# Routing of three batches in a fused attention and mixture-of-experts kernel: element-by-element operations moved from VectorE to GpSimd

## The chip, the cores and the metric

The kernel runs on one core of one Trainium2 chip. The metric is device microseconds (us) for one execution of the whole program. The engines are named as in the profile: PE (TensorE matmul), PEld (its weight loads), DVE (VectorE), ACT (ScalarE), POOL (GpSimd) and SP (SyncE, which only issues DMAs here).

## The reference

Attention with rotary embedding over 4 batches, 8 heads, 576 positions, head size 64; its output, laid out as rows of 512, goes through a router and eight experts. Each token uses one expert, weighted by its probability.

```python
x = attn_out.transpose(0, 2, 1, 3).reshape(B, S, H * D)
logits = np.einsum('bsd,de->bse', x, w_gate)
local_gate = sigmoid(np.einsum('bsd,de->bse', x, w_local))
for b in range(B):
    prev_e = -1
    for s in range(S):
        fresh_e = argmax(logits[b, s])
        e = fresh_e if s == 0 or local_gate[b, s] < 0.5 else prev_e
        prev_e = e
        p = softmax(logits[b, s])
        out[b, s] = p[e] * (relu(x[b, s] @ w1[e]) @ w2[e])
```

## The kernel before

**Attention.** Sixteen pairs of heads are walked in 144 softmax steps, nine to a pair. In a step DVE takes the row minimum `mn` of the scores (L272), PE writes the scores `s` of the next step (L267, two buffers), ACT takes the exponential `e` (L289), PE transposes an earlier `e` (`tm`, L325), ACT copies the transposed tile to its high half `pth` (L303), DVE subtracts it to get the low half `ptl` (L307), and PE multiplies both by the values (`pv`, L361), which ACT and DVE take out to `xt` (L371, L372). Five of the transposed tiles are split by POOL instead (`ON_POOL`, L298 to L300). POOL also does the rotary products (L196, L197) and the splits of queries, keys and values (L206 to L213).

**Routing.** The rows of logits of the first three batches are done together (`route(0, B - 1)`, 15 blocks of 128 tokens), while the last pairs of heads are still in attention; the fourth batch is routed later, under the experts. The parts of the routing are generators; the string `ORDER` gives each a softmax step: `f` finds the expert of each token from the logits (`mx`, `d`, `ex`, `c8`, `f`) and whether it starts anew (`rs`), `r` and `R` carry the last choice forward along the sequence (a transpose `row` and a scan), `e` brings the experts back (`ec`, `e`) and counts them (`cnt`, `oha`, `cox`), `k` ranks each token within its expert (`rk`, `lb`, `lc`, and the one-hot rows `ohr` on POOL), `s` and `p` make the probability, `l`, `x`, `c` plan the first six tiles of 128 tokens, `t` marks which token stands in which slot (`c`, `ex`), `g` gathers their numbers with fifteen matmuls (`idx`, then `ihi`, `gidx`, `ipad`, `sidx` on DVE), `G` issues indirect DMAs that gather the rows of the first four tiles (`x`, L915, on POOL's queue), and `0` and `1` split the first expert weights on POOL (`w_m`, `w_q`, L854 and L855).

**Hand-over.** When attention is done, PE transposes the first gathered tile (`tx`, L926) and starts the products of the experts. From there to the end it is PE that sets the time: `h` (L940) and `o` (L983) follow each other without a gap that matters until the last scatter.

**What sets the order.** PE's order is the order of the code. On DVE, ACT and POOL a scheduler places the instructions at build time; each engine then works through its own list in order, so an instruction that waits holds up all that stand behind it on its engine.

Of the kernel before, what the change touches and what calls it, by code (L numbers as in the profile page):

```python
# [17 lines left out]
ALU = mybir.AluOpType  # L18
# [35 lines left out]

ORDER = ".....fs.rRe.klx.c0pt...wg.1.G"
BIG = 4096.0
# [10 lines left out]
for _n, _w in (  # L67
    ("iota128", 128), ("code8", 8), ("p1", 1),
    ("keys", NBLK * NE), ("s0", NBLK), ("pad", NBLK), ("tok64", NBLK),
    ("scan0", 8 * NG + 8), ("tile128", 25),  # L70
):
    _COLS[_n] = (_off, _off + _w)
    _off += _w
# [3 lines left out]
def _constants():  # L77
# [14 lines left out]
    tok64 = np.zeros((P, NBLK))  # L92
    s0 = np.zeros((P, NBLK))
    pad = np.zeros((P, NBLK))
    s0[0, ::NB] = 1
    pad[:64, 4::NB] = 64
# [5 lines left out]
    put("keys", (TWO23 + 8 * tok[:, :, None] + 7 - np.arange(8)).reshape(P, -1))  # L102
    put("s0", s0)
    put("pad", pad.astype(np.int32))
# [33 lines left out]
def tile_attention_moe(ctx, tc, qk, v, tabs, turn, consts, tri, wg, wts, out):  # L138
# [333 lines left out]
    def route(b0, nb):  # L472

        n = nb * NB
        cs = slice(b0 * NB, b0 * NB + n)
        final = b0 + nb == B
        st = {}

# [3 lines left out]
        def fresh():  # L482
            if final:
                scores(b0)
                yield
            lg = lg_all[:, 0:n]
            mx = blk("mx")
            dve.tensor_reduce(mx, lg[:, :, 0:8], axis=AX.X, op=ALU.max)
            yield
            d = blk("d", 8)  # L490
            dve.tensor_tensor(d, lg[:, :, 0:8], bc(mx, 2, 8), op=ALU.subtract)
            yield
            ex = blk("ex", 8)
# [12 lines left out]
            key = blk("key")  # L506
            dve.tensor_tensor(key, rs, f, op=ALU.mult)
            yield
            st.update(ex=ex, key=key)

# [21 lines left out]
        def experts():  # L532
# [10 lines left out]
            oh = oha[:, cs]  # L543

            dve.tensor_scalar(tcode[:, cs], e, -7.0, 4096.0, op0=ALU.add, op1=ALU.mult)
            cnt = small([P, NE, NG + 1], "cnt", BF16)
            dve.tensor_tensor(cnt[:, :, 1:n + 1].rearrange("p e j -> p j e"), bc(C["code8"], 1, n), bc(e, 2, 8), op=ALU.is_equal)
            dve.tensor_tensor(oh, bc(C["code8"], 1, n), bc(e, 2, 8), op=ALU.is_equal)

            if b0 == 0:  # L550
                dve.memset(cnt[:, :, 0], 0.0)
            else:
                dve.tensor_copy(cnt[:, :, 0], cox_t[0][:, :, NG])
                if n < NG:
# [19 lines left out]

        def probs():
# [15 lines left out]
        def ranks():  # L591
# [45 lines left out]
    def slots(codes, nblk, first, n):  # L637

        st = {}

        def spread_tokens():
# [6 lines left out]
            rhs = rhs.rearrange("p (c j n) -> p c j n", n=n, c=2)  # L648
            dve.tensor_tensor(w, bc(codes(), 1, nblk), bc(tcode[:, 0:nblk], 2, n), op=ALU.is_equal)
# [711 lines left out]
```

## Time and profile before

| what | value |
|---|---|
| median of 3 runs | 546.08 us (544.13 to 546.13) |
| profiled execution: time | 546.83 us |
| profiled execution: span, first to last instruction | 545.1 us |
| granted TensorE clock, mean | 0.994 |
| busy share of the span: PE, DVE, ACT, POOL | 96%, 71%, 63%, 60% |
| routing of the first three batches | about 250 to 293 us |
| first transpose of the experts (`tx`) | 299.62 us |

The busy shares are means over two halves with different limits: in attention, up to about 300 us, PE and DVE are both nearly full; among the experts PE alone is. What a change to the routing does is read in the stretch from 250 to 300 us.

### The profile page before, as it was taken

The page shows a single profiled execution, that of the slowest core. Times are in us where ns is not written, and L with a number is a line of the kernel's source. Part 1 is how long each engine was busy: PE and PEld are TensorE (multiplying, and loading weights), DVE is VectorE, ACT ScalarE, POOL GpSimd, SP SyncE. Part 2 cuts the span into 40 slices and gives each one's busy share as a digit, 9 for nine tenths or more (in the row PEclk, how much of TensorE's full clock was granted, in tenths as well). Part 3 has the DMA queues.
Part 4 walks back from the last instruction along what each step waited for, and adds up shares of the span by engine and source line. Part 5 has one row for each costly group of instructions (what it writes and reads, how often), then busy time and mean ns, then how long its engine had stood idle before and what let it go on. Part 6 is the DMA issues. An engine that isn't in the chain of part 4 may idle for free. (4 is left out here: it accounts for less than half of the span.)

```text
span 545.1 us, 10718 instructions
## 1 busy us (share of the span) xinstructions
PE 521.0 (96%) x3281; PEld 460.4 (84%) x3281; DVE 388.3 (71%) x724; ACT 344.7 (63%) x766; POOL 327.9 (60%) x243
## 2 busy tenths in 40 slices
PE   7989999999999999999999999999999999999992
PEld 3788999999999999998888788887888887888881
DVE  6898999999999999999999935428422635421630
ACT  2799898888998999987676623353523443442440
POOL 2996989878787989887498401337511455411332
PEclk9999999999999999999999999999999999999997
DMA  8759588766877787895289305371647494737340
GB/s 264 284 125 239 166 241 241 152 200 196 245 179 213 204 223 185 209 252 132 57 157 272 86 21 174 115 272 45 227 102 246 123 342 102 247 99 232 87 167 25
DMA packets 63322, 97.37 MB, mean 179 GB/s; under 512 B 28113, under 2 KB 38353, under 8 KB 61458
## 3 DMA queue, kind: packets, MB, share of 16 engines
q1 hardware_dynamic: 60210, 86.84, 56.6%
q0 software_dynamic: 3040, 9.71, 5.5%
q8 instruction: 28, 0.46, 0.4%
q14 instruction: 44, 0.36, 0.2%
HBM read 76.98 MB, written 12.86 MB: 165 GB/s over the span
## 5 line engine op out<-in xcount | busy, mean ns | idle before, releaser
L983 PE MATMUL o<-w,hs 128*128 128x512 f32 x456 | 113.5, 398 | 0.2 <-ACT hs L964 0.2
L272 DVE TENSOR_REDUCE mn<-s 128x1 f32<-128x576 f32 x144 | 107.5, 747 | 3.6 <-PE s L267 2.2
L289 ACT ACTIVATE e<-s,mn 128x576 f32<-128x576 f32 x128 | 95.1, 743 | 18.9 <-DVE mn L272 15.4
L940 PE MATMUL h<-w,xs 128*128 128x512 f32 x444 | 106.2, 393 | 0.9 <-DVE xs L307 0.5
L267 PE MATMUL s<-m,qst 128*128 128x288 f32 x512 | 97.5, 311 | 5.4 <-ACT e L289 3.0
L307 DVE TENSOR_TENSOR ptl<-tm,pth 128x512 fp32r<-128x512 f32 x139 | 95.1, 685 | 6.4 <-ACT pth L303 4.0
L940 PEld LDWEIGHTS h<-w,xs 128*128 128x128 f32 x444 | 82.6, 188 | 19.1 <-DVE w L885 1.2
L983 PEld LDWEIGHTS o<-w,hs 128*128 128x128 f32 x456 | 83.0, 188 | 17.6 <-ACT hs L964 0.6
L989 POOL DMA_INDIRECT out_dram<-os,sidx x19 | 22.8, 1201 | 124.8 <-ACTq L891 71.4
L303 ACT CAST pth<-tm 128x512 fp32r<-128x512 f32 x139 | 80.8, 581 | 12.3 <-PE tm L325 11.2
L267 PEld LDWEIGHTS s<-m,qst 128*128 128x128 f32 x512 | 74.7, 189 | 12.1 <-ACT e L289 6.1
L325 PE MATMUL tm<-wid,e 128*128 128x128 f32 x512 | 77.1, 273 | 1.3 <-ACT e L289 0.5
L196 POOL TENSOR_TENSOR stage<-stage 128x1152 f32<-128x1152 f32 x26 | 68.9, 2665 | 14.0 <-DMA stage<-in_qk_dram 11.9
L361 PE MATMUL pv<-pth,v 128*128 128x288 f32 x256 | 76.4, 314 | 0.4 <-DVE ptl L307 0.2
L361 PE MATMUL pv<-ptl,v 128*128 128x288 f32 x256 | 76.6, 315 | 0.0
L325 PEld LDWEIGHTS tm<-wid,e 128*128 128x128 f32 x512 | 62.0, 140 | 2.2 <-DVE ptl L307 1.0
L885 DVE TENSOR_TENSOR w<-stage,w 128x1024 fp32r<-128x1024 f32 x37 | 50.7, 1403 | 15.7 <-SPq L1049 7.2
L361 PEld LDWEIGHTS pv<-pth,v 128*128 128x128 f32 x256 | 48.3, 189 | 2.8 <-DVE ptl L307 0.9
L361 PEld LDWEIGHTS pv<-ptl,v 128*128 128x128 f32 x256 | 48.4, 189 | 0.0
L307 DVE TENSOR_TENSOR xs<-tx,xs 128x512 fp32r<-128x512 f32 x19 | 13.1, 689 | 41.8 <-ACTq L891 32.2
L307 DVE TENSOR_TENSOR hs<-th,hs 128x512 fp32r<-128x512 f32 x26 | 17.5, 688 | 29.5 <-ACTq L891 17.8
L197 POOL TENSOR_TENSOR stage<-stage 128x576 f32<-128x576 f32 x26 | 36.9, 1432 | 0.2
(198 smaller groups left out, 817.3 us busy)
## 6 DMA issues: line engine op xcount, KB each, us to landing
stage<-in_wts_dram SPq DMA_DIRECT2D x84, 512.0 KB
stage<-in_qk_dram SPq DMA_DIRECT2D x13, 1152.0 KB
qst<-xq SPq DMA_DIRECT2D x56, 128.0 KB
stage<-in_v_dram SPq DMA_DIRECT2D x16, 320.0 KB
m<-xq SPq DMA_DIRECT2D x14, 288.0 KB
m<-xk SPq DMA_DIRECT2D x14, 288.0 KB
m<-xq SPq DMA_DIRECT2D x14, 256.0 KB
m<-xk SPq DMA_DIRECT2D x14, 256.0 KB
```

The costliest lines, as they stand in the source:

```text
L196: engine.tensor_tensor(x, x, tab[:, 2 * f:2 * f + 2], op=ALU.mult)
L197: engine.tensor_tensor(rr[:, f], x[:, 0], x[:, 1], op=ALU.add)
L267: pe.matmul(st[:, h, lo:hi], lhs, keys[:, k0:k0 + hi - lo], start=(n == 0), stop=(n == len(parts_) - 1))
L272: dve.tensor_reduce(mn, s_t[g][:, :, 0:HALF], axis=AX.XY, op=ALU.min)
L289: act.activation(dst.rearrange("p (h s) -> p h s", h=2), s_t.pop(g)[:, :, 0:HALF], AF.Exp, bias=mn, scale=-1.0, accum_out=sums[:, col:col ...
L303: act.copy(hi, src)
L307: dve.tensor_tensor(lo, src, hi.bitcast(F32), op=ALU.subtract)
L325: pe.transpose(ps[:, k], src[:, k * P:(k + 1) * P], ident)
L361: pe.matmul(pv_t[p, u], lhs.rearrange("p c d -> p (c d)"), rhs, start=(n == 0), stop=(n == 9))
L885: (pool if k in on_pool else dve).tensor_tensor(lo, src, hi.bitcast(F32), op=ALU.subtract)
L940: pe.matmul(ps[:, c], xs_t[t][:, x, k], w[y][:, c * 512:(c + 1) * 512], start=(k == 0 and n == 0), stop=(k == 3 and n == 2))
L983: pe.matmul(ps, hs_t[t][:, x, k], w[y][:, (k % 2) * 512:(k % 2 + 1) * 512], start=(k == 0 and n == 0), stop=(k == 7 and n == 2))
```

## The change

Within the routing of the first three batches, operations that go element by element and read SBUF alone are issued on POOL; the reductions, the scans, whatever reads PSUM, and the short chain that plans the tiles stay on DVE. A fused instruction becomes two on POOL (compare, then multiply). One addition goes to ACT. Two parts are cut in two, so that what uses a result of POOL stands a softmax step later: `F` (maximum and key) after `f`, and `E` (the scan of the counts) after `e`. Both take free places of `ORDER`; the other parts keep theirs. The fourth batch stays on DVE.

```diff
-ORDER = ".....fs.rRe.klx.c0pt...wg.1.G"
+ORDER = ".....fFsrReEklx.c0pt...wg.1.G"
...
+        some = dve if final else pool
...
-            dve.tensor_tensor(d, lg[:, :, 0:8], bc(mx, 2, 8), op=ALU.subtract)
+            some.tensor_tensor(d, lg[:, :, 0:8], bc(mx, 2, 8), op=ALU.subtract)
...
-            dve.scalar_tensor_tensor(c8, d, 0.0, keys, op0=ALU.is_equal, op1=ALU.mult)
-            dve.scalar_tensor_tensor(rs, lg[:, :, 8], ZTHR, C["s0"][:, cs], op0=ALU.is_lt, op1=ALU.max)
-            yield
+            if final:
...
+            else:
+                pool.tensor_scalar(c8, d, 0.0, None, op0=ALU.is_equal)
+                pool.tensor_tensor(c8, c8, keys, op=ALU.mult)
+                pool.tensor_scalar(rs, lg[:, :, 8], ZTHR, None, op0=ALU.is_ge)
+                pool.tensor_tensor(rs, rs, C["later"][:, cs], op=ALU.mult)
+            yield
+            st.update(ex=ex, c8=c8, rs=rs)
+
+        def resets():
+            c8, rs = st["c8"], st["rs"]
             f = blk("f")
             dve.tensor_reduce(f, c8, axis=AX.X, op=ALU.max)
             yield
             key = blk("key")
-            dve.tensor_tensor(key, rs, f, op=ALU.mult)
...
+                pool.tensor_tensor(rs, rs, f, op=ALU.mult)
+                pool.tensor_tensor(key, f, rs, op=ALU.subtract)
...
-            dve.tensor_scalar(tcode[:, cs], e, -7.0, 4096.0, op0=ALU.add, op1=ALU.mult)
-            dve.tensor_tensor(cnt[:, :, 1:n + 1].rearrange("p e j -> p j e"), bc(C["code8"], 1, n), bc(e, 2, 8), op=ALU.is_equal)
-            dve.tensor_tensor(oh, bc(C["code8"], 1, n), bc(e, 2, 8), op=ALU.is_equal)
+            if not final:
+                whole, e, far = e, blk("p"), blk("c8", 8)
+                pool.tensor_copy(e, whole)
+                pool.tensor_tensor(far, bc(C["code8"], 1, n), bc(e, 2, 8), op=ALU.subtract)
+            for x in (cnt[:, :, 1:n + 1].rearrange("p e j -> p j e"), oh):
+                if final:
+                    dve.tensor_tensor(x, bc(C["code8"], 1, n), bc(e, 2, 8), op=ALU.is_equal)
+                else:
+                    pool.tensor_scalar(x, far, 0.0, None, op0=ALU.is_equal)
+            some.tensor_scalar(tcode[:, cs], e, -7.0, 4096.0, op0=ALU.add, op1=ALU.mult)
...
+        def counts():
+            cnt = st["cnt"]
             cox = small([P, NE, NG + 1], "cox", BF16, bufs=2)
...
-            dve.tensor_scalar(se, se, 1e-9, None, op0=ALU.add)
+                act.add(se, se, 1e-9)
...
-            dve.tensor_tensor(p, p, st["se"], op=ALU.mult)
+            some.tensor_tensor(p, p, st["se"], op=ALU.mult)
...
-            dve.tensor_tensor(o, r, hi, op=ALU.subtract)
+            some.tensor_tensor(o, r, hi, op=ALU.subtract)
...
+                pool.tensor_scalar(hi, hi, -TWO23, None, op0=ALU.add)
+                pool.tensor_tensor(tcode[:, cs], hi, tcode[:, cs], op=ALU.add)
                 for j in range(n):
                     pool.tensor_scalar(ohr[:, b0 * NB + j], C["iota128"], o[:, j:j + 1], None, op0=ALU.is_equal)
             yield
-            dve.scalar_tensor_tensor(tcode[:, cs], hi, -TWO23, tcode[:, cs], op0=ALU.add, op1=ALU.add)
...
+            if first == 0:
+                far = small([P, nblk * n], "d").rearrange("p (j n) -> p j n", n=n)
+                pool.tensor_tensor(far, bc(codes(), 1, nblk), bc(tcode[:, 0:nblk], 2, n), op=ALU.subtract)
+                pool.tensor_scalar(w, far, 0.0, None, op0=ALU.is_equal)
...
-            dve.tensor_tensor(rhs[:, 0], w, bc(C["tok64"][:, 0:nblk], 2, n), op=ALU.mult)
-            dve.tensor_scalar(rhs[:, 1], w, C["p1"], None, op0=ALU.mult)
+            some.tensor_tensor(rhs[:, 0], w, bc(C["tok64"][:, 0:nblk], 2, n), op=ALU.mult)
+            some.tensor_scalar(rhs[:, 1], w, C["p1"], None, op0=ALU.mult)
```

DVE's list becomes 14 instructions shorter, POOL's 21 longer, ACT's one longer. Three places of the lists show how they move.

**DVE, start of the routing.** Before, from the maximum `mx` of the logits to the second softmax minimum behind it:

```order
L488 TENSOR_REDUCE mx_4214<-lg_all 128x15
L501 SCALAR_TENSOR_TENSOR rs_4222<-lg_all,cst 128x15
L430 RECIPROCAL sum_3604<-sum_3604 128x10
L491 TENSOR_TENSOR d_4216<-lg_all,mx_4214 128x120
L272 TENSOR_REDUCE mn_4231<-s_4194 128x1
L499 SCALAR_TENSOR_TENSOR c_6_4220<-d_4216,cst 128x120
L307 TENSOR_TENSOR ptl_3983<-tm_4201,pth_3982 128x4x128
L504 TENSOR_REDUCE f_4224<-c_6_4220 128x15
L567 TENSOR_REDUCE se_4273<-ex_4218 128x15
L507 TENSOR_TENSOR key_4226<-rs_4222,f_4224 128x15
L272 TENSOR_REDUCE mn_4280<-s_4233 128x1
```

Now, the same place (`c_6` is `c8`, written by POOL; `ex` is written by ACT from `d`, which POOL writes):

```order
L489 TENSOR_REDUCE mx_4214<-lg_all 128x15
L430 RECIPROCAL sum_3604<-sum_3604 128x10
L272 TENSOR_REDUCE mn_4229<-s_4194 128x1
L591 TENSOR_REDUCE se_4310<-ex_4218 128x15
L515 TENSOR_REDUCE f_4271<-c_6_4220 128x15
L307 TENSOR_TENSOR ptl_3983<-tm_4201,pth_3982 128x4x128
L272 TENSOR_REDUCE mn_4279<-s_4231 128x1
```

Four instructions have left the stretch, and `f`, which reads what POOL writes, now stands ahead of the `ptl` and the `mn`.

**DVE, the counts.** Now, from the experts `e` to the second `mn` behind them (`cnt` and `d`, the products of probabilities, come from POOL):

```order
L555 SCALAR_TENSOR_TENSOR e_4411<-ec_4405,cst 128x15
L372 TENSOR_TENSOR xt_4338<-pv_1_4369,tmp_4339 64x288
L272 TENSOR_REDUCE mn_4457<-s_4427 128x1
L583 SCALAR_TENSOR_TENSOR cox_4452<-cst,cnt_4413 128x128
L607 TENSOR_REDUCE p_4748<-d_4746 128x15
L307 TENSOR_TENSOR pkl_4290<-tk_4441,pkh_4289 128x256
L272 TENSOR_REDUCE mn_4516<-s_4459 128x1
```

Before, `tcode`, `cnt`, `oha` and `cox` stood between `xt` and the first `mn`, and `p` stood behind the second.

**POOL, towards the gathers.** Now, from the split of the last values to the gathers of the first four tiles (`w_m`, `w_q` are the first expert weights):

```order
L213 TENSOR_TENSOR v_15_4342<-stage,v_15_4342 128x10x64
L681 TENSOR_TENSOR d_4793<-code_4684,tcode 128x90
L682 TENSOR_SCALAR c_30_4791<-d_4793 128x90
L687 TENSOR_TENSOR ex_4792<-c_30_4791,cst 128x90
L688 TENSOR_SCALAR ex_4792<-c_30_4791,cst 128x90
L889 TENSOR_SCALAR w_m<-stage 128x1024
L890 TENSOR_TENSOR w_m<-stage,w_m 128x1024
L889 TENSOR_SCALAR w_q_4915<-stage 128x1024
L890 TENSOR_TENSOR w_q_4916<-stage,w_q_4915 128x1024
L950 DMA x_4926<-rows_d,gidx 128x513 x4
```

The four instructions between the values and the weights are new here; ahead of them, around the `ohr` of the ranks, stand three more new ones (`lc`, `lb`, `tcode`).

## Rows read from the trace of the kernel before

**Rows 1.** Windows: busy time of each engine (and instructions), clock, DMA share, GB/s.

```profile
250.00:261.00 11.00, 9.41 (x69) 7.99 (x66) 10.78 (x24) 7.96 (x21) 5.79 (x6) 1.00 0.59 135
261.00:272.00 11.00, 10.19 (x80) 9.46 (x80) 10.47 (x25) 7.66 (x18) 5.78 (x7) 1.00 0.16 29
272.00:290.00 18.00, 16.95 (x122) 15.20 (x122) 17.69 (x48) 12.12 (x31) 17.62 (x24) 1.00 0.83 196
```

**Rows 2.** Timeline of PE: start, duration, instruction, and the idle time before it.

```profile
253.69 0.80 PE L267 MATMUL s<-m,qst 128*128 128x288 f32 x4 [0.94 <-ACT e L289]
...
268.14 1.03 PE L267 MATMUL s<-xk,qtail 128*128 128x288 f32 x6 [0.81 <-issue]
```

**Rows 3.** Timeline of DVE, the four longest routing instructions that leave it.

```profile
250.47 1.36 DVE L501 SCALAR_TENSOR_TENSOR rs<-lg_all,cst 128x15 f32<-128x15 f32 x1
...
264.14 1.16 DVE L545 TENSOR_SCALAR tcode<-e 128x15 f32<-128x15 int32 x1
...
271.42 0.99 DVE L607 TENSOR_TENSOR lc<-rk,lb 128x15 f32<-128x15 f32 x1
...
283.25 0.99 DVE L652 TENSOR_TENSOR ex<-c,cst 128x90 bf16<-128x90 bf16 x1
```

**Rows 4.** Timeline of POOL in the same stretch.

```profile
249.38 0.27 POOL L468 TENSOR_TENSOR lg_all<-gm 128x45 f32<-128x45 f32 x1
...
249.62 0.67 POOL L206 TENSOR_SCALAR xq<-stage 128x576 fp32r<-128x576 f32 x1
250.38 1.42 POOL L207 TENSOR_TENSOR xq<-stage,xq 128x576 fp32r<-128x576 f32 x1
...
263.98 1.28 POOL L300 TENSOR_TENSOR ptl<-stage,pth 128x512 fp32r<-128x512 f32 x1
266.06 0.51 POOL L577 TENSOR_TENSOR d<-ex,oha 128x120 f32<-128x120 f32 x1 [0.79 <-DVE oha L548]
...
272.52 8.75 POOL L612 TENSOR_SCALAR ohr<-cst,lc 128x128 bf16<-128x128 f32 x15
...
282.64 0.25 POOL L728 TENSOR_SCALAR after<-take 128x8 f32<-128x8 f32 x1
```

**Rows 5.** Timeline of DVE: `f`, the scan of the counts, and the minimum behind it.

```profile
253.55 0.27 DVE L504 TENSOR_REDUCE f<-c 128x15 f32<-128x120 f32 x1
...
265.91 0.42 DVE L558 TENSOR_TENSOR_SCAN cox<-cst,cnt 128x128 bf16<-128x128 f32 x1
266.36 0.76 DVE L272 TENSOR_REDUCE mn<-s 128x1 f32<-128x576 f32 x1
```

**Rows 6.** Timeline of POOL up to the first gather.

```profile
285.73 1.05 POOL L854 TENSOR_SCALAR w_m<-stage 128x1024 fp32r<-128x1024 f32 x1
286.86 2.38 POOL L855 TENSOR_TENSOR w_m<-stage,w_m 128x1024 fp32r<-128x1024 f32 x1
...
290.34 2.36 POOL L855 TENSOR_TENSOR w_q<-stage,w_q 128x1024 fp32r<-128x1024 f32 x1
293.02 1.26 POOL L915 DMA_INDIRECT x<-rows_d,gidx  x1 [0.32 <-DVE sidx L672]
```

**Rows 7.** Timeline of DVE, the numbers that the gathers need.

```profile
292.20 0.53 DVE L668 CAST gidx<-ihi 128x6 uint32<-128x6 f32 x1
...
292.83 0.17 DVE L672 SCALAR_TENSOR_TENSOR sidx<-ipad,ihi 128x6 uint32<-128x6 f32 x1
```

**Rows 8.** Timeline of PE at the hand-over to the experts.

```profile
290.41 0.53 PE L661 MATMUL idx<-ex,ohr 128*128 128x12 bf16 x15
...
293.75 0.37 PE L361 MATMUL pv<-pth,v 128*128 128x288 f32 x1 [0.22 <-DVE ptl L307]
...
299.62 0.60 PE L926 MATMUL tx<-wid,x 128*128 128x128 f32 x4
```

**Rows 9.** Gathers `x`, issue to landing: the third, then the fifth and sixth.

```profile
DMA to landing us min/median/max: 5.5/5.5/5.5
...
DMA to landing us min/median/max: 3.7/3.7/3.7
```

More of the change, by code (lines that the diff above doesn't have):

```diff
@@ L68 @@
     ("iota128", 128), ("code8", 8), ("p1", 1),
-    ("keys", NBLK * NE), ("s0", NBLK), ("pad", NBLK), ("tok64", NBLK),
+    ("keys", NBLK * NE), ("later", NBLK), ("pad", NBLK), ("tok64", NBLK),
     ("scan0", 8 * NG + 8), ("tile128", 25),
@@ L92, in _constants @@
     tok64 = np.zeros((P, NBLK))
-    s0 = np.zeros((P, NBLK))
+    later = np.ones((P, NBLK))
     pad = np.zeros((P, NBLK))
-    s0[0, ::NB] = 1
+    later[0, ::NB] = 0
     pad[:64, 4::NB] = 64
@@ L102, in _constants @@
     put("keys", (TWO23 + 8 * tok[:, :, None] + 7 - np.arange(8)).reshape(P, -1))
-    put("s0", s0)
+    put("later", later)
     put("pad", pad.astype(np.int32))
@@ L498, in fresh @@
             keys = C["keys"].rearrange("p (j e) -> p j e", e=NE)[:, cs]
-            dve.scalar_tensor_tensor(c8, d, 0.0, keys, op0=ALU.is_equal, op1=ALU.mult)
             rs = blk("rs")
-            dve.scalar_tensor_tensor(rs, lg[:, :, 8], ZTHR, C["s0"][:, cs], op0=ALU.is_lt, op1=ALU.max)
+            if final:
+                dve.scalar_tensor_tensor(c8, d, 0.0, keys, op0=ALU.is_equal, op1=ALU.mult)
+                dve.scalar_tensor_tensor(rs, lg[:, :, 8], ZTHR, C["later"][:, cs], op0=ALU.is_ge, op1=ALU.mult)
+            else:
[3 more added lines that the diff above has]
+                pool.tensor_tensor(rs, rs, C["later"][:, cs], op=ALU.mult)
             yield
+            st.update(ex=ex, c8=c8, rs=rs)
+        def resets():
+            c8, rs = st["c8"], st["rs"]
             f = blk("f")
@@ L506, in fresh @@
             key = blk("key")
-            dve.tensor_tensor(key, rs, f, op=ALU.mult)
+            if final:
+                dve.scalar_tensor_tensor(key, rs, 0.0, f, op0=ALU.is_equal, op1=ALU.mult)
+            else:
+                pool.tensor_tensor(rs, rs, f, op=ALU.mult)
+                pool.tensor_tensor(key, f, rs, op=ALU.subtract)
             yield
-            st.update(ex=ex, key=key)
+            st["key"] = key
         def last_reset(part):
@@ L556, in experts @@
             yield
+            st["cnt"] = cnt
+        def counts():
+            cnt = st["cnt"]
             cox = small([P, NE, NG + 1], "cox", BF16, bufs=2)
@@ L562, in experts @@
             cox_t[b0] = cox
-            st["cnt"] = cnt
         def sums():
@@ L568, in sums @@
             yield
-            dve.tensor_scalar(se, se, 1e-9, None, op0=ALU.add)
+            if final:
+                dve.tensor_scalar(se, se, 1e-9, None, op0=ALU.add)
+            else:
+                act.add(se, se, 1e-9)
             yield
@@ L606, in ranks @@
             yield
-            dve.tensor_tensor(o, r, hi, op=ALU.subtract)
+            some.tensor_tensor(o, r, hi, op=ALU.subtract)
             if final:
                 dve.tensor_tensor(ohr[:, cs], bc(C["iota128"], 1, n), bc(o, 2, P), op=ALU.is_equal)
-            else:
+                yield
+                dve.scalar_tensor_tensor(tcode[:, cs], hi, -TWO23, tcode[:, cs], op0=ALU.add, op1=ALU.add)
+            else:
+                pool.tensor_scalar(hi, hi, -TWO23, None, op0=ALU.add)
+                pool.tensor_tensor(tcode[:, cs], hi, tcode[:, cs], op=ALU.add)
                 for j in range(n):
@@ L613, in ranks @@
             yield
-            dve.scalar_tensor_tensor(tcode[:, cs], hi, -TWO23, tcode[:, cs], op0=ALU.add, op1=ALU.add)
-            yield
-        parts = [fresh, lambda: last_reset(0), lambda: last_reset(1), experts, ranks]
+        first, second = (lambda: last_reset(0)), (lambda: last_reset(1))
         if final:
-            return parts[:4] + [sums, probs] + parts[4:] + later()
-        order = dict(f=fresh, r=parts[1], R=parts[2], e=experts, k=ranks, s=sums, p=probs, **early())
+            return [fresh, resets, first, second, experts, counts, sums, probs, ranks] + later()
+        order = dict(f=fresh, F=resets, r=first, R=second, e=experts, E=counts, k=ranks, s=sums, p=probs, **early())
         return [None if c == "." else order[c] for c in ORDER]
@@ L639, in slots @@
         st = {}
+        some = pool if first == 0 else dve
         def spread_tokens():
```

5 lines of the change are left out of this document (4 added, 1 removed).

## The prediction

> **What bounds the kernel now.** I read the busy table first, then the windows, then the waits, then the timelines of the engines from 250 to 300 us. Among the experts PE runs without a gap that matters, so what happens before 300 us is kept to the end unless something at the hand-over takes it back. In the routing stretch DVE is the fullest engine: 10.78 of 11.00 us, 10.47 of 11.00, 17.69 of 18.00 [rows 1]. PE there has idle time: 1.59, 0.81 and 1.05 us, together 3.45 us [rows 1]. The two longest gaps stand in front of a score product: 0.94 us, ended by an exponential `e` on ACT, which follows a late minimum on DVE, and 0.81 us [rows 2]. So the most that a faster DVE can give back before the hand-over is about 3.4 us.
>
> DVE is full partly because it waits while it is counted busy. Four instructions of 15 or 90 elements a row take 1.36, 1.16, 0.99 and 0.99 us [rows 3], where the same kind takes 0.17 us elsewhere (`sidx` [rows 7]). `rs` ends at 250.47 + 1.36 = 251.83, and POOL's L207 at 250.38 + 1.42 = 251.80; `tcode` ends at 265.30, POOL's L300 at 263.98 + 1.28 = 265.26 [rows 3, 4]. An instruction of DVE with operands in SBUF alone, issued while POOL is at a tile, ends with POOL's instruction. The ones that leave DVE are such instructions, so the change takes the right ones from it.
>
> **The change part by part.** I follow the order of time.
>
> *Fresh experts.* From DVE go `rs` (1.36 us), `d`, `c8` and `key`, in all some 1.7 us of its time. But `f` now stands in front of `ptl` and `mn` on DVE and waits for `c8` from POOL. POOL ends `lg_all` at 249.65 and then does `rs` (two instructions), L206, `d`, L207 and `c8` (two), in this order. Prices on POOL: a small single-input instruction 0.25, a small two-input one 0.27, one of 128x120 with two inputs 0.51, L206 0.67, L207 1.42 [rows 4]; the single-input one of 128x120 I put at 0.3, between 0.25 and the 0.58 of one `ohr` (8.75 / 15 [rows 4]). Sum: 0.25 + 0.27 + 0.67 + 0.51 + 1.42 + 0.3 + 0.51 = 3.9, so `c8` is there at about 253.6. Before, `f` started at 253.55 [rows 5]. DVE thus spends the 1.7 us waiting, and the `ptl` that used to stand ahead of `f` comes behind it. Gain here: 0, bounds +0.6 us of loss (one `ptl`) and 0.9 of gain (the gap at 253.69, if POOL is quicker).
>
> *Counts.* Three instructions of DVE (`tcode` alone 1.16 us) leave the place between `xt` and `mn`, so this `mn`, which started at 266.36 [rows 5], can start some 2 us earlier. Behind it `cox` waits for `cnt` from POOL. There the cast of `e` gets in just ahead of the L300 of 263.98, whose 1.28 us then pass, and then come `far` (0.51), `tcode` (0.25) and `cnt` (0.3 to 0.58): `cnt` stands at about 265.26 + 0.25 + 0.51 + 0.25 + 0.4 = 266.7, `cox` ends near 267.1 where it ended at 266.33 [rows 4, 5]. The matmuls of the ranks come 0.45 us later, but the gap of 0.81 us behind them closes, since the exponential it hung on is 2 us earlier. Then `p` waits for POOL's `d` (0.3 + 0.51 later) and holds up the next `mn` by some 0.7 us. Net on PE: 0.4 us gained, bounds -0.4 and +0.8.
>
> *Ranks to slots.* `lc` (0.99 us), and later both `ex`, leave DVE, which hereby comes about 1 us earlier through the dense stretch of the tile plans, and another 2 us near 283 to 287. PE has 1.05 us of idle time there [rows 1] and can take up most of it: 0.9 us, bounds 0.4 and 1.05. So PE reaches the matmuls of `idx`, at 290.41 before [rows 8], about 1.3 us earlier.
>
> *POOL's list.* In 272 to 290 POOL is busy for 17.62 of 18.00 us [rows 1], one instruction behind the other, and at its end stand the weights `w_m`, `w_q` and then the first gather [rows 6]. New in this list are `lc`, `lb` and `tcode` (0.27 + 0.25 + 0.27), and `far`, `c` and twice `ex` (0.4 + 0.27 + 0.4 + 0.3 to 0.58; a two-input one of 90 I put between the 0.27 for 45 elements of `lg_all` and the 0.51 for 120). Sum 2.3 us, bounds 2.0 and 2.6. Nothing covers it: the copy by ACT that the last L300 ahead of `ohr` waits for follows the same exponentials as before, so the start moves by half a microsecond at most. `w_q` ends at 290.34 + 2.36 + 2.3 = 295.0, and the first gather, which went out at 293.02, goes at about 295.3 with its old gap of 0.3 [rows 6]. This is the price of the change. `idx` itself has its `ex` at about 288, before PE wants it.
>
> *Hand-over.* `tx` waits for three things. PE's own list: 299.62 - 1.3 = 298.3. The first tile `x`: 295.3 plus 3.7 us (a gather with none ahead of it) or 5.5 us (the third in a row) [rows 9]. The first has none ahead but shares the DMA queues with loads of weights; I take 4.6, the middle, so 299.9, and with the start of the weight load about 300.1. Last, DVE: `gidx`, `ipad` and `sidx` have their operands in SBUF alone, and behind them on DVE stands the `ptl` for which the last `pv` wait [rows 7, 8]. They come at about 291 now, into the middle of POOL's weights, where before only the end of one caught `gidx` (0.53 us, until 292.73 [rows 7]). If `gidx` waits for the end of `w_m` (291.7) and `ipad` for the first half of `w_q` (292.7), `sidx` gets through at 293.0, where it was; if `sidx` is caught as well, it ends at 295.2, 2.2 us later. I take the first for the sum. The latest of the three decides: 300.1 against 299.62.
>
> **Sum.** Gain before the hand-over 0 + 0.4 + 0.9 = 1.3 us; it turns into a wait in front of `tx`, which starts 0.5 us later than before: +0.5 us. The profiled execution took 546.83 us (span 545.1), 0.75 above the median of the runs shown; against the median it gives 546.08 + 0.5 = 546.6 us.
>
> **A rule to weigh.** The rows above show DVE's small instructions ending with POOL's [rows 3, 4]. The Trainium skill, "SBUF — State Buffer", section "Who interferes with whom", says why: GpSimd and VectorE share one pair of SBUF ports, held for a whole instruction, and a VectorE instruction that copies or scales in a 2-port mode, or has two inputs in SBUF, blocks until GpSimd's is through. By that rule all three instructions of the index chain are caught, and the sum would be +2.2 us, 548.3; this is rival C.
>
> **The rivals.**
>
> *A, the forecast: gains given back at the hand-over.* From -1.3 (PE's own list decides because the gather lands early) to +1.3 us (5.5 us to landing: 300.8). Chance 0.62.
>
> *B, faster: the time of DVE comes through.* For it: DVE is the fullest engine in all three windows, and the waits on POOL's tiles fall away. Against it: DVE waits for POOL at `f`, `cox` and `p`. It decides if POOL gets `c8` out before 252.5, that is if small instructions cost half as much there, and if the list to the gather grows by less than 1 us. Then PE's 3.45 us come back, less up to 1: -3.4 to -1.5 us, 542.7 to 544.6. Chance 0.15.
>
> *C, slower: the index chain is caught behind POOL's weights.* `sidx` ends at 295.2, the `ptl` behind it 0.7 us later, and `pv`, at 293.75 before, starts at 295.9; `tx` comes 5.87 us behind it as before [rows 8], at 301.8: +2.2 us, and up to +3.3 if the new list of POOL is 1 us longer than I put it. For it: every case in rows 3. Against it: no row shows two such instructions in a row under a full POOL. It decides if `gidx` starts before the first half of `w_q` does. 548.3 to 549.4. Chance 0.23.
>
> *D, no effect.* That DVE's time is off the path is no case of its own: it ends in A, near 0.
>
> **How the numbers follow.** I put the point at A's 546.6. The range takes in the larger part of B and all but the top of C: 543.8 to 549.2. About 0.5%, 2.7 us, is what a measurement of this kernel can tell from no change. Faster by more than that: B's upper part and a little besides, 0.12; slower by more: the upper half of C and a little, 0.16; within: 0.72.
>
> **What would show it.** Right: in the profile after, `f` has idle time in front of it that POOL ends; `cox` and `p` too; the gap of PE at 253.69 stays near 1 us in some form, that at 268 shrinks; the first gather goes out 2 to 2.6 us after 293.02; PE waits in front of `tx` or in front of the last `pv`. Wrong: `f` starts before 252.7; POOL has idle time between `ohr` and the gather; or `tx` starts before 298.5.

## The result and the profile after

| what | before | after |
|---|---|---|
| median of all runs | 545.07 us (12 runs) | 548.4 us (12 runs, 547.06 to 550.49) |
| profiled execution: time, span | 546.83, 545.1 us | 548.26, 546.4 us |
| granted TensorE clock, mean | 0.994 | 0.992 |

The changed kernel takes 1.0058 times as long as the one before, 95% interval [1.0045, 1.0071]: slower by 3.3 us, where the prediction said 0.5. The time lies inside its range (543.8 to 549.2 us), but a slowdown of more than 2.7 us had only a chance of 0.16. That it lies inside is in part luck: the forecast started from 546.08 us, a median of three runs, and over twelve the kernel before takes 545.07; as a change, the range ended at +3.1 us. The slowdown is above all of rival A's range (-1.3 to +1.3 us) and at the top of rival C's (+2.2 to +3.3), though not by C's way, as the rows below show. One run of the kernel before, timed beside e9 to e11, took 732.72 us at a mean granted clock of 0.654 and is in no ratio.

The two profiles don't start the routing at the same moment: `lg_all`, its first instruction on POOL, stands at 247.96 in the trace after and at 249.38 in the one before [rows 4]. Rows below are quoted as they are; where I compare, I add these 1.42 us and say "shifted".

**The routing stretch.** Windows of the changed kernel, the columns as in [rows 1]:

```profile
250.00:261.00 11.00, 9.28 (x67) 7.80 (x66) 8.50 (x17) 8.03 (x21) 6.65 (x9) 1.00 0.63 143
261.00:272.00 11.00, 10.26 (x78) 9.31 (x77) 8.39 (x22) 7.92 (x19) 8.28 (x15) 1.00 0.17 21
272.00:290.00 18.00, 17.77 (x146) 16.29 (x145) 16.74 (x45) 14.76 (x36) 17.59 (x28) 1.00 0.85 207
...
308.00:312.00 4.00, 2.61 (x13) 1.50 (x14) 3.68 (x9) 1.69 (x4) 0.04 (x1) 1.00 0.23 69
312.00:316.00 4.00, 4.00 (x13) 2.86 (x14) 2.50 (x3) 0.00 (x0) 0.00 (x0) 0.57 0.01 2
```

DVE (third pair of numbers) is busy for 8.50, 8.39 and 16.74 us instead of 10.78, 10.47 and 17.69 [rows 1], and for 8.35, 8.39 and 16.87 us in windows moved by the 1.42 us; POOL (fifth) stays full in the third window. The two windows below the dots are spoken of further down. DVE's timeline shows where the freed time went:

```profile
252.28 0.28 DVE L515 TENSOR_REDUCE f<-c 128x15 f32<-128x120 f32 x1 [1.74 <-POOL c L506]
...
265.74 0.42 DVE L583 TENSOR_TENSOR_SCAN cox<-cst,cnt 128x128 bf16<-128x128 f32 x1 [2.10 <-POOL cnt L568]
266.42 0.28 DVE L607 TENSOR_REDUCE p<-d 128x15 f32<-128x120 f32 x1 [0.26 <-POOL d L604]
...
289.55 1.29 DVE L703 CAST gidx<-ihi 128x6 uint32<-128x6 f32 x1
290.76 0.16 DVE L705 TENSOR_SCALAR ipad<-ihi 128x6 f32<-128x6 f32 x1
290.95 0.89 DVE L707 SCALAR_TENSOR_TENSOR sidx<-ipad,ihi 128x6 uint32<-128x6 f32 x1
...
302.73 4.43 DVE L920 TENSOR_TENSOR w<-stage,w 128x1024 fp32r<-128x1024 f32 x3
...
311.13 0.68 DVE L307 TENSOR_TENSOR xs<-tx,xs 128x512 fp32r<-128x512 f32 x1
```

The stalls of [rows 3] have become waits at `f`, `cox` and `p`, as forecast.

**POOL, up to the first gather and the weight split behind the gathers:**

```profile
264.77 0.93 POOL L568 TENSOR_SCALAR cnt<-c 128x120 bf16<-128x120 f32 x1
...
271.62 0.22 POOL L634 TENSOR_TENSOR lc<-rk,lb 128x15 f32<-128x15 f32 x1
...
288.46 2.36 POOL L890 TENSOR_TENSOR w_m<-stage,w_m 128x1024 fp32r<-128x1024 f32 x1
290.78 1.05 POOL L889 TENSOR_SCALAR w_q<-stage 128x1024 fp32r<-128x1024 f32 x1
291.91 2.38 POOL L890 TENSOR_TENSOR w_q<-stage,w_q 128x1024 fp32r<-128x1024 f32 x1
294.46 1.27 POOL L950 DMA_INDIRECT x<-rows_d,gidx  x1 [0.17 <-DMA stage<-in_wts_dram]
...
301.39 2.42 POOL L920 TENSOR_TENSOR w<-stage,w 128x1024 fp32r<-128x1024 f32 x1
```

The first gather goes out at 295.88 shifted, 2.86 us after 293.02 [rows 6].

**PE, its waits from 291 us on, up to the transpose of the third tile:**

```profile
292.49 0.40 PE L361 MATMUL pv<-pth,v 128*128 128x288 f32 x1 [1.85 <-DVE ptl L307]
...
299.43 0.63 PE L961 MATMUL tx<-wid,x 128*128 128x128 f32 x4 [0.86 <-DMA x<-rows_d,gidx]
...
307.92 1.09 PE L1009 MATMUL th<-wid,hr 128*128 128x128 f32 x8 [0.68 <-ACT hr L981]
309.27 1.60 PE L975 MATMUL h<-w,xs 128*128 128x512 f32 x4 [0.26 <-ACT xs L303]
311.87 1.12 PE L975 MATMUL h<-w,xs 128*128 128x512 f32 x2 [1.00 <-DVE xs L307]
312.78 1.05 PE L538 MATMUL row<-wid,key 128*1 128x128 f32 x4
313.49 5.25 PE L975 MATMUL h<-w,xs 128*128 128x512 f32 x18
318.57 0.27 PE L538 MATMUL row<-wid,key 128*1 128x128 f32 x1
318.68 0.60 PE L961 MATMUL tx<-wid,x 128*128 128x128 f32 x4
```

The same place in the kernel before, PE's timeline:

```profile
310.99 0.73 PE L940 MATMUL h<-w,xs 128*128 128x512 f32 x2 [0.54 <-DVE xs L307]
311.56 0.60 PE L523 MATMUL row<-wid,key 128*1 128x128 f32 x4
311.91 4.35 PE L940 MATMUL h<-w,xs 128*128 128x512 f32 x18
316.10 0.27 PE L523 MATMUL row<-wid,key 128*1 128x128 f32 x1
316.21 0.60 PE L926 MATMUL tx<-wid,x 128*128 128x128 f32 x4
```

From the resumed `h` to the third `tx` PE needs 316.21 - 310.99 = 5.22 us before and 318.68 - 311.87 = 6.81 us after, for the same matmuls. The last two windows above say why (the last number but two is the granted clock): after a stretch in which PE was busy for 2.61 of 4.00 us, the granted clock is 0.57, that is mostly the lower of its two levels (1.2 against 2.4 GHz). In the kernel before it is 1.00 there, as in all its windows from 250 to 324 us:

```profile
308.00:312.00 4.00, 3.04 (x19) 2.25 (x20) 3.79 (x7) 2.05 (x5) 0.00 (x0) 1.00 0.36 127
312.00:316.00 4.00, 4.00 (x20) 3.28 (x19) 1.62 (x2) 0.00 (x0) 0.00 (x0) 1.00 0.00 2
```

**Where the time is lost.** Distance behind before, in shifted time: the first `tx` 299.43 + 1.42 - 299.62 = 1.23 us; the resumed `h` 311.87 + 1.42 - 310.99 = 2.30; the third `tx` 318.68 + 1.42 - 316.21 = 3.89. From the fourth to the fourteenth tile the distance stays at 3.84 or 3.85. So all is lost before 319 us, in three pieces: 1.23 up to the first `tx`, 1.07 up to the second tile's `h`, 1.59 at the lower clock. These are pieces of one pair of executions: at the end of the span 2.72 us are left of them (546.4 + 1.42 - 545.1), since what follows the last product is 0.9 us shorter there, and the medians of twelve differ by 3.3.

### The profile page after: what moved, and what is told of

Read it like the earlier page. It is cut to its first block, busy times and chain, and to the rows that moved or that the text cites. A ratio compares the mean times of both kernels' runs of the same rounds, so it can differ in the third digit from the quotient of the medians.

```text
span 546.4 us, 10727 instructions
## 1 busy us (share of the span) xinstructions
PE 522.0 (96%) x3281; PEld 460.6 (84%) x3281; DVE 382.6 (70%) x710; ACT 345.1 (63%) x767; POOL 333.6 (61%) x263
## 5 line engine op out<-in xcount | busy, mean ns | idle before, releaser
L975 PE MATMUL h<-w,xs 128*128 128x512 f32 x444 | 107.6, 396 | 1.7 <-DVE xs L307 1.0
```

What stands on the lines that cost most here:

```text
L975: pe.matmul(ps[:, c], xs_t[t][:, x, k], w[y][:, c * 512:(c + 1) * 512], start=(k == 0 and n == 0), stop=(k == 3 and n == 2))
```

## The experiments

Twelve kernels, each timed beside the kernel before on the same chip (medians of before there: 545.44, 545.23, 544.30 and 545.33 us). The ratio is that of the comparison on record; it differs from the ratio of the two medians by up to 0.1%. "Third `tx`" is its distance behind that of before, in the profiled execution, each trace shifted so that `lg_all` stands at 249.38.

| kernel | median us | ratio to before, 95% | first gather (shifted) | third `tx` |
|---|---|---|---|---|
| changed kernel | 548.4 | 1.0058 [1.0045, 1.0071] | 295.88 | +3.89 |
| e1 slots on DVE | 548.23 | 1.0042 [1.0024, 1.0060] | 296.01 | +2.99 |
| e2 gathers first | 549.44 | 1.0075 [1.0056, 1.0095] | 292.64 | +4.79 |
| e3 fresh on DVE | 547.47 | 1.0035 [1.0021, 1.0049] | 295.51 | +1.94 |
| e4 before, more on POOL | 549.18 | 1.0063 [1.0043, 1.0083] | 295.32 | +3.84 |
| e5 counts on DVE | 547.34 | 1.0045 [1.0028, 1.0062] | 295.35 | +2.15 |
| e6 less on POOL | 546.74 | 1.0028 [1.0012, 1.0045] | 294.30 | +1.35 |
| e7 before, less on POOL | 545.72 | 1.0014 [1.0000, 1.0029] | 293.77 | +0.75 |
| e8 filler | 547.15 | 1.0031 [1.0019, 1.0044] | 295.90 | +2.34 |
| e9 index on POOL | 548.82 | 1.0076 [1.0060, 1.0091] | 297.06 | +3.73 |
| e10 first gather ahead | 549.59 | 1.0100 [1.0073, 1.0128] | 292.57 | +4.68 |
| e11 both | 548.23 | 1.0061 [1.0041, 1.0081] | 294.23 | +3.90 |
| e12 slots alone, values on DVE | 551.75 | 1.0111 [1.0092, 1.0131] | 298.65 | +5.70 |

**e1: the slots part undone** (`c`, `ex`, `ex`).

```diff
-        some = pool if first == 0 else dve
+        some = dve
...
-                pool.tensor_tensor(far, bc(codes(), 1, nblk), bc(tcode[:, 0:nblk], 2, n), op=ALU.subtract)
-                pool.tensor_scalar(w, far, 0.0, None, op0=ALU.is_equal)
+            dve.tensor_tensor(w, bc(codes(), 1, nblk), bc(tcode[:, 0:nblk], 2, n), op=ALU.is_equal)
```

> The changed kernel with one part undone: the four operations that mark which token stands in which slot (c and both ex) are on VectorE again. GpSimd's list between the values and the first weights is 1.7 us shorter (0.36 + 0.44 + 0.34 + 0.55 in the profile of the changed kernel), VectorE has some 2 us more to do near 283 to 287 us. Theory T (GpSimd's list is what costs: it delays the first gather and the weights behind it): most of the loss goes, 545.0 to 546.6 us, first gather 1.5 us earlier against the start of the routing. Rival R (the loss is made earlier, where VectorE waits for GpSimd at f, cox and p): no better than the changed kernel, 548.0 to 549.5 us.

The rival's range, and a miss for the theory as I had put it. `w_m` did start 1.8 us earlier (286.95 against 288.75, both shifted), but the instructions that came back to DVE stalled there, and the minimum behind them was late. DVE's timeline of e1:

```profile
284.64 0.47 DVE L682 TENSOR_TENSOR ex<-c,cst 128x90 bf16<-128x90 bf16 x1
285.04 1.52 DVE L683 TENSOR_SCALAR ex<-c,cst 128x90 bf16<-128x90 bf16 x1
```

PE's timeline of e1 has the wait that follows, and a granted clock of 0.57 stands in the window behind it:

```profile
288.25 1.33 PE L267 MATMUL s<-m,qst 128*128 128x288 f32 x4 [2.58 <-ACT e L289]
```

So this part does take a stall from DVE, as the change intends; undone in this order of DVE's list, it costs as much as it gives. The loss is another one than in the changed kernel: 2.97 of its 2.99 us are there at the first `tx`, and DVE's weight splits take 3.49 us as before the change.

**e2: all four gathers ahead of `w_q`.**

```diff
-ORDER = ".....fFsrReEklx.c0pt...wg.1.G"
+ORDER = ".....fFsrReEklx.c0pt...wg.G.1"
```

> The changed kernel, with the first four gathers issued ahead of the second half of the early weights (G and 1 change places in ORDER); no work is added or removed. T: the first gather goes out some 2 us earlier, sidx meets no w_q, the transpose of the first tile no longer waits: 545.5 to 547.3 us. R: unchanged, 548.0 to 549.0 us. A third way: w_q now comes late for the second group of products of the first expert, and the time stays at 548 with PE waiting there instead.

The first `tx` came 0.43 us earlier than in the kernel before, without a wait, and yet the time went up, to just above the rival's range. PE's timeline of e2:

```profile
310.39 1.91 PE L975 MATMUL h<-w,xs 128*128 128x512 f32 x4 [1.61 <-ACT xs L303]
312.99 1.22 PE L975 MATMUL h<-w,xs 128*128 128x512 f32 x2 [0.69 <-DVE xs L307]
```

DVE's three weight splits that follow the first tile took 6.13 us here, 4.43 in the changed kernel and 3.49 before. The clock then falls to 0.50 in 312 to 316 us, and from the resumed `h` to the third `tx` PE takes 320.69 - 312.99 = 7.70 us, 2.48 more than before. What POOL has to do had only been moved from in front of the first tile to in front of the second.

**e3: the fresh part undone** (`d`, `c8`, `rs`, `key`).

```diff
-                pool.tensor_scalar(c8, d, 0.0, None, op0=ALU.is_equal)
-                pool.tensor_tensor(c8, c8, keys, op=ALU.mult)
-                pool.tensor_scalar(rs, lg[:, :, 8], ZTHR, None, op0=ALU.is_ge)
-                pool.tensor_tensor(rs, rs, C["later"][:, cs], op=ALU.mult)
+            dve.scalar_tensor_tensor(c8, d, 0.0, keys, op0=ALU.is_equal, op1=ALU.mult)
+            dve.scalar_tensor_tensor(rs, lg[:, :, 8], ZTHR, C["later"][:, cs], op0=ALU.is_ge, op1=ALU.mult)
```

> The changed kernel with another part undone: the fresh experts (d, c8, rs, key) are on VectorE again, so that f no longer waits for GpSimd. GpSimd's list towards the gathers is the same as in the changed kernel. T: little changes, 547.4 to 548.8 us, for the gather goes out as late as before. R: the wait of 1.74 us in front of f goes, and the time falls to 546.5 us or less.

Inside the theory's range. PE reached `idx` at 288.75 (shifted), a little before the 289.18 of the changed kernel: moving this part had gained nothing. Its `tx` comes as late (at 300.80 shifted, behind 1.19 us of idle time). From its resumed `h` to the third `tx` it takes 318.05 - 312.82 = 5.23 us (both unshifted), as the kernel before does, since no window here shows a lower clock.

**e4: the kernel before, with six subtractions of 128x90 more on POOL ahead of the weights**, whose results nothing uses.

```diff
+                far = small([P, nblk * n], "d").rearrange("p (j n) -> p j n", n=n)
+                for _ in range(6):
+                    pool.tensor_tensor(far, bc(codes(), 1, nblk), bc(tcode[:, 0:nblk], 2, n), op=ALU.subtract)
```

> The kernel before, with nothing moved: VectorE does all that it did, and GpSimd gets six more operations of 128x90 (about 2.3 us) in front of the early weights, whose result nobody reads. T: GpSimd's list alone makes the loss: 2.0 to 3.5 us above the kernel before, 547 to 548.6 us. R: GpSimd has room there: within 0.8 us of the kernel before.

With a list on POOL that is 2.49 us longer, and nothing taken from DVE or PE, the kernel before becomes as slow as the changed one, 0.6 us beyond the theory's range. The way is another one, that of rival C: 3.76 of its 3.84 us are there at the first `tx`. DVE's timeline of e4:

```profile
291.10 0.87 DVE L672 CAST gidx<-ihi 128x6 uint32<-128x6 f32 x1
291.88 0.16 DVE L674 TENSOR_SCALAR ipad<-ihi 128x6 f32<-128x6 f32 x1
292.07 2.32 DVE L676 SCALAR_TENSOR_TENSOR sidx<-ipad,ihi 128x6 uint32<-128x6 f32 x1
294.32 1.28 DVE L307 TENSOR_TENSOR ptl<-tm,pth 128x512 fp32r<-128x512 f32 x2
```

and POOL's:

```profile
290.91 1.04 POOL L858 TENSOR_SCALAR w_q<-stage 128x1024 fp32r<-128x1024 f32 x1
292.03 2.34 POOL L859 TENSOR_TENSOR w_q<-stage,w_q 128x1024 fp32r<-128x1024 f32 x1
```

`gidx` ends with the short half of `w_q`, `sidx` comes 0.04 us after the start of the long half and ends with it, at 295.17 shifted (C: 295.2), and PE waits 2.72 us for the `ptl` behind it: `pv` starts at 295.92 shifted (C: 295.9). From there to `tx` PE takes 7.46 us, where C had 5.87, with a granted clock of 0.63 in 296 to 300 us.

**e5: the counts part undone** (`far`, `cnt`, `oha`, `tcode`).

```diff
-                    pool.tensor_scalar(x, far, 0.0, None, op0=ALU.is_equal)
-            some.tensor_scalar(tcode[:, cs], e, -7.0, 4096.0, op0=ALU.add, op1=ALU.mult)
+                dve.tensor_tensor(x, bc(C["code8"], 1, n), bc(e, 2, 8), op=ALU.is_equal)
+            dve.tensor_scalar(tcode[:, cs], e, -7.0, 4096.0, op0=ALU.add, op1=ALU.mult)
```

> The changed kernel with its counts part (cast, far, cnt, oha, tcode) back on DVE; the rest stays on POOL. Theory (the loss is made at the hand-over, by POOL's list between 271 and 296 us being too long): these operations sit at 262 to 266 us, where POOL has idle time behind them until lc, so the list to the first gather does not get shorter and the time stays with the changed kernel's 548.4: 547.6 to 549.2. Rival (the loss is made in the routing stretch, where cox waits 2.10 us for POOL's cnt): that wait goes, and the time falls to 547.0 or less.

The median falls between the two ranges and the interval takes in the changed kernel's, so the time decides nothing. The trace speaks for the theory: the first `tx` is as late as in the changed kernel (+1.25 us). Its low clock (0.57) stands in 292 to 296 us, in the stretch where the changed kernel's PE still has a wait for `x` ahead; the `tx` of e5 has none.

**e6: the changed kernel with one tile split less on POOL; e7: the same in the kernel before.**

```diff
-ON_POOL = (125, 129, 130, 132, 134)
+ON_POOL = (125, 129, 130, 132)
```

> The changed kernel with one split of a transposed softmax tile less on POOL (the one at 281 to 284 us, 0.61 + 1.28 us); DVE does it, one more ptl of 0.68 us. Theory (POOL's list up to the first gather makes the loss): the first gather goes out 1.5 to 1.9 us earlier, the waits in front of pv, tx and h shrink by 1.5 to 2 us, and with them the stretch of half clock behind them may go: 545.0 to 547.2. Rival (DVE and PE themselves are late, POOL is covered): no gain, and DVE has more to do: 547.8 to 549.4.

> The kernel before with the same one split moved from POOL to DVE. Theory: in the kernel before, PE waits only 0.69 and 0.54 us around tx and h, so a shorter list of POOL has little to give, and DVE, full there, gets 0.68 us more: 544.6 to 546.2, against 545.1 for the kernel before. Rival (POOL's list bounds the hand-over before the change too): 543.0 to 544.4.

Both times lie in the theory's ranges. In e6 the first gather goes out 1.58 us earlier, POOL's weight split ends just as DVE's begin (300.62 + 2.39 = 303.01, against 302.93), DVE's three take 3.49 us again, and no low clock follows. DVE's timeline of e6:

```profile
302.93 3.49 DVE L920 TENSOR_TENSOR w<-stage,w 128x1024 fp32r<-128x1024 f32 x3
```

What is left of its loss, 1.22 of 1.35 us at the first `tx`, is at DVE: the split that it took over makes PE wait in PE's timeline of e6:

```profile
279.24 0.80 PE L267 MATMUL s<-m,qst 128*128 128x288 f32 x4 [1.68 <-ACT e L289]
```

e7 has such a wait too (1.40 us) and is 0.75 us behind its own parent at the third `tx`; it is slower than before by 0.14%, hardly more than nothing.

**e8: four matmuls more on PE, in the wait ahead of the second tile's third pass.** They repeat the first two and the sum is begun anew behind them.

```diff
+            if t == 1 and k == 0:
+                for _ in range(2):
+                    for c in range(2):
+                        pe.matmul(ps[:, c], xs_t[t][:, 0, k], w[0][:, c * 512:(c + 1) * 512], start=True, stop=True)
```

> The changed kernel with four matmuls more of PE, in the wait of 1.00 us ahead of the second tile's third pass (311.87 us): the first two matmuls are done twice over and their sum begun anew, so nothing else is changed. Theory (besides the waits themselves, the idle time of PE around 308 to 312 us is answered by a granted clock of 0.57 in 312 to 316, which costs some 2 us): PE is busy in the wait, the clock stays at 1.00, and the time falls by 1.2 to 2.2 us although PE has 1 us more to do: 546.0 to 547.3. Rival (the low clock costs nothing real, or comes from the earlier waits): 548.0 to 549.6.

The waits ahead are those of the changed kernel (1.84 and 0.84 us at `pv` and `tx`), DVE's splits take 4.45 us, and `h` resumes at the same moment (313.32 against 313.29, shifted). Only PE's busy time and the clock differ. Windows of e8:

```profile
308.00:312.00 4.00, 3.25 (x17) 2.33 (x17) 3.76 (x9) 1.69 (x4) 0.13 (x1) 1.00 0.30 79
312.00:316.00 4.00, 4.00 (x20) 3.19 (x21) 2.40 (x3) 0.00 (x0) 0.00 (x0) 1.00 0.01 2
```

and PE's timeline of e8:

```profile
311.95 0.73 PE L979 MATMUL h<-w,xs 128*128 128x512 f32 x2 [0.49 <-DVE xs L307]
...
317.18 0.60 PE L961 MATMUL tx<-wid,x 128*128 128x128 f32 x4
```

From the resumed `h` to the third `tx`: 5.23 us instead of 6.81. So the low clock costs 1.58 us, and in this execution useless work took it away; five of the twelve executions of e8 still have a mean granted clock of 0.991 or 0.992, the others 0.996 or 0.997. The median fell by 1.25 us, from 1.0058 of before to 1.0031; the two intervals just fail to touch.

**e9: the index chain on POOL, between `w_m` and `w_q`.** `sidx` becomes two instructions.

```diff
-            dve.tensor_copy(gidx[:, first:first + n], hi)
+            some.tensor_copy(gidx[:, first:first + n], hi)
...
-            dve.scalar_tensor_tensor(sidx[:, first:first + n], pad, -1.0, hi, op0=ALU.add, op1=ALU.add)
+                pool.tensor_tensor(pad, pad, hi, op=ALU.add)
+                pool.tensor_scalar(sidx[:, first:first + n], pad, -1.0, None, op0=ALU.add)
```

> The changed kernel with the index chain (gidx, ipad, sidx) on POOL, between w_m and w_q, so that no instruction of it is caught on DVE behind POOL's weights and the ptl for pv comes at once. Theory (the wait in front of pv only gives back what PE had gained, and the first gather at the end of POOL's list decides after it): pv starts 1 to 1.8 us earlier, the gather 0.7 to 1 us later because POOL has four small instructions more, and tx waits the longer for x: 547.8 to 549.8, against 548.4. Rival (the index chain caught on DVE is what costs): the time falls to 547.0 or less.

Inside the theory's range. `pv` has no wait and starts 2.08 us earlier than in the changed kernel (291.83 against 293.91, shifted), and all of it turns into a longer wait for the gather, which goes out 1.18 us later; `tx` comes 0.83 us later than in the changed kernel. PE's timeline of e9:

```profile
301.23 0.68 PE L965 MATMUL tx<-wid,x 128*128 128x128 f32 x4 [3.80 <-DMA x<-rows_d,gidx]
```

**e10: the gather of tile 0 alone ahead of `w_q`; e11: e9 and e10 together.**

```diff
-wg.1.G"
+wg.H1G"
...
+                "H": lambda: gathers([0]), "G": lambda: gathers([1, 2, 3]),
```

> The changed kernel with the gather of tile 0 alone ahead of w_q on POOL's list; w_q comes 1.6 us later, the other three gathers and everything behind them stay where they were. Theory (tx waits for x_0, and what POOL does behind it waits for the same list): the wait of 0.86 us in front of tx goes, the wait of 1.85 us in front of pv stays, and the waits of the second tile stay or grow by a few tenths; without a drop of the clock 546.0 to 547.3, with it 547.4 to 548.2. Rival (the later w_q takes all of it back): 548.3 to 549.6.

> The changed kernel with both: index chain on POOL, and the gather of tile 0 alone ahead of w_q. Theory: pv waits no more, x_0 is there in time, and PE comes to tx 1.5 to 2.7 us earlier than in the changed kernel; a part of it is given back in front of the second tile, whose weights and gather POOL still has late: 545.2 to 547.2. Rival (what POOL does behind the first gather decides, whenever tx starts): 548.0 to 549.6.

Both land in the rival's range. The first `tx` comes 0.51 and 1.09 us earlier than in the kernel before, and by the third both are 4.68 and 3.90 us behind. PE's timeline of e11:

```profile
311.18 0.73 PE L979 MATMUL h<-w,xs 128*128 128x512 f32 x2 [2.07 <-DVE w L924]
312.91 0.83 PE L979 MATMUL h<-w,xs 128*128 128x512 f32 x2 [1.00 <-DVE xs L307]
```

Whichever of POOL's jobs is put first, the one put last holds up PE; and behind these waits too the clock falls (0.67 in 312 to 316 us).

**e12: the candidate.** e3 and e5 together, and the low half of the last values on DVE.

```diff
-        pool.tensor_tensor(v2[:, :, 1], src, v2[:, :, 0].bitcast(F32), op=ALU.subtract)
+        (dve if p == NPAIR - 1 else pool).tensor_tensor(v2[:, :, 1], src, v2[:, :, 0].bitcast(F32), op=ALU.subtract)
```

> The changed kernel with its fresh part and its counts part back on DVE, so that only ranks and slots are on POOL, and with the low half of the last pair's values (L213, 1.57 us of POOL's list at 283.9 us) on DVE. It is meant as the version with the best chance of beating the kernel before. Theory (POOL's list between 271 us and the first gather decides at the hand-over): the list is 1.6 us shorter than in the changed kernel, the first gather goes out near 294 on the clock of the rows before, the weights behind it no longer catch DVE, and no drop of the clock follows: 544.8 to 546.3, against 545.1 for the kernel before. Rival (the value split on DVE at 281 us holds up the next minimum, and PE waits 1 to 2 us there, as it did when a tile split was moved): 546.4 to 547.6.

Slower than either range, by a blunder of mine that DVE's timeline of e12 shows:

```profile
282.99 0.82 DVE L213 TENSOR_TENSOR v<-stage,v 128x640 fp32r<-128x640 f32 x1 [7.28 <-POOL v L212]
```

The low half needs the high half, which POOL makes behind fourteen `ohr`; DVE waited 7.28 us for it with the next minima behind, and PE 6.57. It says nothing on the theory. None of the twelve beats the kernel before.

## Why the prediction was off by 2.8 us, step by step

- **Fresh experts: right.** `c8` was put at 253.6, and `f` started at 253.70 shifted, with 1.74 us of idle time that POOL ended. e3, which reaches `idx` 0.43 us earlier without this part, speaks for a gain of 0 or a small loss, inside the bounds.
- **Counts: right, one term mis-sized.** `cnt` with its scattered output took 0.93 us, not 0.3 to 0.58, so `cox` ended at 267.58 shifted, where I had 267.1. The gap of 0.81 us [rows 2] went down to one of 0.53.
- **Ranks to slots, and PE's gain: right.** `idx` was put 1.3 us earlier; it came 1.23 us earlier (289.18 shifted, 290.41 before [rows 8]).
- **POOL's list: right in kind, 0.56 us too short.** Forecast +2.3, measured +2.86. The four instructions of the slots take from 285.41 to 287.33, 1.92 us with the time between them, and `lc` starts half a microsecond later than the first `ohr` did; the text allowed for that half microsecond and did not add it. The first gather, expected 2 to 2.6 us after 293.02, is thus 0.26 us outside that. POOL has 20 instructions more (263 against 243 in the profiles), not 21 as the section on the change has it.
- **The index chain: right in its time.** `gidx` ends with `w_m` and `sidx` with the first half of `w_q`, at 293.26 shifted (293.0 forecast); the forecast had `ipad` wait there, and it took 0.16 us. The rule of the Trainium skill that was weighed there ("SBUF — State Buffer", "Who interferes with whom") agrees with these rows for `gidx` and `sidx`. `ipad` started at 290.76, just as POOL went from `w_m` to `w_q` (290.78), so its row cannot tell whether it would have been held. The sum that I made by the rule, with the chain behind all of `w_q`, did not come about here. In e4 it did: `sidx` started 0.04 us behind the start of the second half of `w_q`, in the changed kernel 0.96 us ahead of it. So rival C was a matter of one microsecond, and the sign that was to decide it pointed the wrong way: `gidx` started ahead of the first half of `w_q` in the changed kernel (289.55 against 290.78), without C, and behind it in e4 (291.10 against 290.91), with C. e9 shows that in the changed kernel the wait at `pv` (1.85 us) costs nothing of itself, since `tx` waits for the gather behind it.
- **Hand-over: the step that failed.** "The latest of the three decides: 300.1 against 299.62." The first `tx` came at 300.85; of the 0.75 us between, 0.56 is POOL's list. But the real error is that the sum ends there. I had written that among the experts PE runs without a gap that matters, so that what happens before 300 us is kept to the end, and two more payments stood behind it.
- **First, POOL's next weight split.** Behind the gathers POOL splits another weight. Before, it ended at 302.99, just as DVE began its own three; POOL's and DVE's timelines of the kernel before:

```profile
300.61 2.38 POOL L885 TENSOR_TENSOR w<-stage,w 128x1024 fp32r<-128x1024 f32 x1
```

```profile
302.90 3.49 DVE L885 TENSOR_TENSOR w<-stage,w 128x1024 fp32r<-128x1024 f32 x3
...
310.25 0.69 DVE L307 TENSOR_TENSOR xs<-tx,xs 128x512 fp32r<-128x512 f32 x1
```

  Now it ends at 303.81, 1.08 us behind the start of DVE's first; that one takes 2.16 us and the other two 1.21, together 4.43 us: 0.94 more. Overlap and extra time go together in the other kernels: 0.09 us and none in the kernel before, 0.08 and none in e6, 0.75 and 0.62 in e3, 0.93 and 0.80 in e5. DVE has no idle time that matters from there to the second tile's `xs`, so `h` waits for that. 1.23 + 0.94 = 2.17 of the 2.30 us at the resumed `h`.
- **Second, the clock.** PE's idle pieces around 308 to 312 us are answered by a lower granted clock, 1.58 us (e8). The prediction had no term for it; nothing in the trace of before showed a window under 1.00 here.

The three pieces (first `tx`, extra time of DVE's three splits, extra time from the resumed `h` to the third `tx`) add up to 1.23 + 0.94 + 1.59 = 3.76 of the 3.89 us in the changed kernel, and in the others as well: 1.25 + 0.96 + 0.01 = 2.22 of 2.34 in e8, 1.18 + 0.62 + 0.01 = 1.81 of 1.94 in e3, 1.25 + 0.80 = 2.05 of 2.15 in e5, 1.22 of 1.35 in e6, and -0.43 + 2.64 + 2.48 = 4.69 of 4.79 in e2.

That POOL's list is the cause is shown from both sides: lengthening it alone in the kernel before (e4) gives a loss of the same size, though by rival C's way and a low clock behind it; shortening it in the changed one (e6) takes out the second and third piece and about half of the loss (1.0028 instead of 1.0058); and moving its order about (e2, e10, e11) moves the wait but does not take the loss away. That the time fell at the top of C's range is luck: C's chain was not what cost. Rival B failed at its own condition: `c8` was not out before 252.5 (253.66 shifted), and the list grew by more than 1 us.

What stays open: what makes the clock fall. In the profiled executions e3, with waits of 0.68 and 1.00 us at the same places, kept it, while the changed kernel, with 0.68, 0.26 and 1.00, did not. But it is not the same in every execution of a kernel: the mean granted clock of e3 is 0.991 or 0.992 in eight of twelve and 0.995 or 0.996 in four, the profiled one among these; that of the changed kernel is 0.993 or less in ten of twelve and 0.995 or 0.996 in two. So the third piece is read from one execution, and how much of the 3.3 us it makes in the median is not shown beyond e8's 1.25 us. And whether some order of DVE's list lets e6's gain come without its wait at 279 us was not tried.

## What to carry to other kernels

Before work is moved to an idle-looking engine, read that engine's list up to the next thing that others wait for: POOL was busy for 60% of the span, and full for the 18 us that mattered. Follow a delay past the first wait that it makes, to everything that stands behind it on the same queue, here a second weight split; a sum that stops at the first meeting point is too small. And where the matmul engine is the bound, count its idle pieces twice over: once as time, and once for the lower clock that may follow.

## What the runs showed of the hardware

- A few waits close together cost PE more than their length: with 2.61 of 4.00 us busy, the granted clock fell to 0.57 in the next window, 1.58 us more for 20 matmuls of `h` and five of `row`; with four matmuls of no use in one of the waits it was 1.00. Both are profiled executions; others of the same kernel can differ.
- Under a full POOL, a small instruction of DVE that was caught ended with the instruction of POOL that ran at that moment, not later: `gidx` 1.29, `sidx` 0.89 us in one kernel, 0.87 and 2.32 in another, by where they fell. A weight split of DVE (1.21 us by itself) took 2.16 us when POOL's was still at work for 1.08 us of it.
- On POOL a 128x120 comparison took 0.52 us into a dense tile and 0.93 us into a scattered one of bf16; POOL began the next one 0.56 us behind the start of the latter, so what waited for the result paid, not POOL's list.
